# A fused LayerNorm, sliding-window attention and gated FFN kernel: 512-query chunks, a hand-set instruction order, resident weights, and the output projection summed in PSUM

## The chip, the cores and the metric

The kernel runs on one core of one Trainium2 chip. The metric is the device time of one execution in microseconds, and lower is better. A profile is of one execution, and the measured time lies about 2 us above its span (first to last instruction).

Engines are named as the profile names them: PE is TensorE, DVE VectorE, ACT ScalarE, POOL GpSimd and SP SyncE. PEclk is the clock that the throttle granted to PE, as a share of full speed.

## The reference, cut to what matters

One token sequence of 2048 x 512 is normalised. The result feeds windowed attention (32 heads of 16 columns, each query sees its own and the 255 preceding keys) and a gated FFN without a nonlinearity. Both halves and the input are summed. All tensors are bfloat16.

```python
def _layernorm(x, axis=-1, eps=1e-5):
    m = jnp.mean(x, axis=axis, keepdims=True)
    v = jnp.var(x, axis=axis, keepdims=True)
    return (x - m) / jnp.sqrt(v + eps)

def _A_ref(x, wqkv, wo):                      # wqkv (512, 1536), wo (512, 512)
    H = 32; Dh = D // H; W = 256
    ...
    mask = (idx[:, None] - idx[None, :] >= 0) & (idx[:, None] - idx[None, :] < W)
    scores = jnp.where(mask[None, None], scores * (Dh ** -0.5), -1e9)   # condensed
    p = _softmax(scores, axis=-1)
    ...                                        # p @ v, heads joined, @ wo

def _B_ref(x, w_gate, w_up, w_down):           # F = 1792
    return ((x @ w_gate) * (x @ w_up)) @ w_down          # condensed

xn = _layernorm(A_x)
return A_x + _A_ref(xn, A_wqkv, A_wo) + _B_ref(xn, B_w_gate, B_w_up, B_w_down)
```

## The kernel before

The attention walks over blocks of 128 keys. For each block, four heads at a time, it computes the scores of 128 keys against 384 queries, takes exp on ACT, and cuts the two triangular masks on POOL. The value matmuls follow one group later. LayerNorm, projection and FFN units are emitted between those steps. A scheduler of the framework decides the final order of each engine; attention has high priority. The code is condensed: cuts are marked by "...", and lines that only allocate tiles are left out.

```python
    def ln_stats_chunks(self, Tlist):           # four blocks of 128 rows at once
        ...
                nc.vector.bn_stats(out=st[:], in_=xc[:, b, :])
                nc.vector.bn_aggr(out=self.mv_all[:, tb, :], in_=st[:])
        nc.scalar.activation(out=std[:, tb0:tb1], in_=self.mv_all[:, tb0:tb1, 1], func=ACT.Sqrt, ...)
        nc.vector.reciprocal(out=self.rstd_all[:, tb0:tb1], in_=std[:, tb0:tb1])

    def lnproj_block(self, tb, xnT):            # Q and K: 128 matmul columns at a time
        ...
        for c in range(4):
            for k in range(4):
                nc.tensor.matmul(ps[:, c, :], lhsT=W[:, k, 128 * c:128 * c + 128],
                                 rhs=xnT[:, k, 128 * b:128 * b + 128], start=(k == 0), stop=(k == 3))
        nc.scalar.activation(out=self.Q[:, :, tok], in_=ps[:], func=ACT.Copy)
        ...

    def ffn_gu_group(self, T, xnT, hT, fg, gsize):   # weights loaded again for each chunk
        ...
        wg = self.wstream.tile([128, 4, 128 * gsize], BF16, tag="wg")
        nc.sync.dma_start(out=wg[:, :, 0:ncol], in_=self.B_wg[...])
        ...

    def ffn_down_block(self, T, hT, b):         # FFN half goes to DRAM
        ...
        nc.vector.tensor_tensor(out=y0[:], in0=psd[:], in1=xb[:], op=ALU.add)
        nc.sync.dma_start(out=self.y0_d[128 * tb:128 * tb + 128, :], in_=y0[:])

    def attn_scores_group(self, hp, t, c, par, km):
        Nq = min(384, self.S - 128 * t)
        S = self.psum.tile([128, 4, 512], F32, tag="S", name="S", bufs=1)
        for e in range(4):
            ...                                  # one matmul of Nq columns on 16 or 32 rows
            nc.tensor.matmul(S[:, e, 0:Nq], lhsT=lhsT, rhs=rhs, start=True, stop=True,
                             tile_position=(32 * e, 0))
        nc.scalar.activation(out=P[:, :, 0:Nq], in_=S[:, :, 0:Nq], func=ACT.Exp, scale=0.25)
        nc.gpsimd.affine_select(out=P[:, :, 0:128], ...)
        if Nq == 384:
            nc.gpsimd.affine_select(out=P[:, :, 256:384], ...)

    def final_block(self, tb):                  # attention half goes to DRAM
        ...
        nc.vector.tensor_copy(out=att[:], in_=outp[:])
        nc.sync.dma_start(out=self.attn_d[128 * tb:128 * tb + 128, :], in_=att[:])

    def combine_block(self, tb, e1=None, e2=None):   # both halves come back
        e1.dma_start(out=a[:], in_=self.attn_d[128 * tb:128 * tb + 128, :])
        e2.dma_start(out=y[:], in_=self.y0_d[128 * tb:128 * tb + 128, :])
        nc.vector.tensor_tensor(out=r[:], in0=a[:], in1=y[:], op=ALU.add)
        nc.sync.dma_start(out=self.out_flat[128 * tb:128 * tb + 128, :], in_=r[:])
    ...
                self.pending.append((hp, t, heads))
                if len(self.pending) > 1:        # values one group behind scores
                    self.attn_pv(*self.pending.pop(0))       # condensed
```

The softmax here doesn't subtract the row's maximum and nothing guards it: scores larger than these inputs give would overflow.

## Time and profile before

| | before |
|---|---|
| time, median of 3 runs | 375.51 us (374.96 to 377.72) |
| span of the profile | 372.9 us |
| PE busy | 309.6 us, 83% |
| first score matmul starts, last matmul ends | 29.05 us, 357.7 us |

The page gives the busy time of each engine, and then, for 40 slices of the span, the busy share in tenths (here the rows of PE and of its granted clock):

```profile
PE 309.6 (83%) x3340; PEld 161.4 (43%) x3392; DVE 186.6 (50%) x390; ACT 201.5 (54%) x170; POOL 154.9 (42%) x256
...
PE   0187888998998898889999999999999989999930
PEclk9999899999999999999999999999999999999985
```

PE is the busiest engine by far. It is not full in the first three slices and in the last two. In between the digits 8 are short waits. The clock is nearly full throughout.

A record's length overlaps its neighbours (a matmul of 512 columns is recorded with 378 ns, and the next one starts 215 ns after it), so PE's work is better read from start-to-start distances in the timeline: 215 ns for a matmul of 512 columns, 56 ns for 128 columns, 25 ns for a value matmul of 17 columns, and about 370 ns for a score group. Times the counts, that is about 291 us.

Among the groups of instructions (busy time, mean ns, then idle time before them and what ended it) two lines matter:

```profile
L209 ACT ACTIVATE P<-S 128x1536 bf16<-128x1536 f32 (+2 forms) x128 | 175.4, 1370 | 90.5 <-PE S L206 73.1
L236 PE MATMUL acc<-Vaug,P 128*128 128x17 bf16 x1440 | 60.8, 171 | 16.4 <-POOL P L210 12.8
```

ACT's exp waits for PE (73.1 of its 90.5 us of idle time), so ACT isn't the bound. The value matmuls make PE wait 16.4 us in all, mostly for POOL's mask.

The chain of waits shows the start and the end. Its columns are start, length and what the time was spent on:

```profile
1.84 14.99 DMA xc<-in_A_x_dram
...
353.74 2.05 DMA attn_d<-att
...
356.33 3.11 DMA a<-attn_d
...
366.39 3.35 DMA a<-attn_d
```

The load in the first line is that of the second input chunk, which lands at 16.8 us; the first chunk had landed by 4.2 us. DVE's timeline shows how PE comes to depend on it:

```profile
16.85 0.69 DVE L101 BATCH_NORM_STATS2 st<-xc 128x6 f32<-128x512 bf16 x1 [7.16 <-DMA xc<-in_A_x_dram]
```

The statistics of the second chunk stand in DVE's order ahead of the copy that PE's first projection needs, so DVE waits 7.16 us and PE 7.9 us. At the end the attention half of each block goes out to DRAM and comes back before the sum.

### The profile page before, as it was taken

What the parts mean: (1) busy time and instruction counts of PE and PEld (TensorE: products, weight loads), DVE (VectorE), ACT (ScalarE), POOL (GpSimd) and SP (SyncE); (2) the same over time, 40 slices, a digit from 0 to 9 for tenths busy, and PEclk for the clock granted to TensorE, in tenths of its full rate; (3) what the DMA queues carried; (4) which work ended last, traced back from release to release, by engine and by line L of the source; (5) the groups of instructions that cost most, each with busy time, mean ns of one, the idle gap of its engine ahead of it and who ended that gap; (6) DMA issues with size and microseconds to landing.
All of it is one profiled execution on the core that took longest, in us unless ns stands there. A gap on an engine that the chain in (4) does not pass through costs nothing.

```text
span 372.9 us, 8075 instructions
## 1 busy us (share of the span) xinstructions
PE 309.6 (83%) x3340; PEld 161.4 (43%) x3392; DVE 186.6 (50%) x390; ACT 201.5 (54%) x170; POOL 154.9 (42%) x256
## 2 busy tenths in 40 slices
PE   0187888998998898889999999999999989999930
PEld 0164654454554445554434444444434444454410
DVE  3265465454546323355556434665664466667421
ACT  1029788767772674657566666666675446520000
POOL 4002545555552442535445555455564445330011
PEclk9999899999999999999999999999999999999985
DMA  7930012122014001011243212422333364442254
GB/s 287 335 95 3 7 53 58 35 80 58 6 54 114 26 4 59 30 56 58 59 113 88 78 49 71 129 87 72 98 104 99 110 193 153 123 124 77 70 156 153
DMA packets 46196, 33.81 MB, mean 91 GB/s; under 512 B 2544, under 2 KB 44912, under 8 KB 46160
## 3 DMA queue, kind: packets, MB, share of 16 engines
q1 hardware_dynamic: 44592, 29.63, 26.6%
q0 software_dynamic: 848, 3.02, 2.5%
q10 hardware_dynamic: 720, 0.66, 0.6%
q8 instruction: 26, 0.43, 0.5%
q14 instruction: 10, 0.08, 0.1%
HBM read 27.00 MB, written 6.29 MB: 89 GB/s over the span
## 4 chain that ended last, share of the span: by engine, by line
PE 45%; ACT 23%; DMA 10%; POOL 9%; DVE 6%; issue 5%; SPq 1%; ACTq 0%; DVEq 0%; POOLq 0%
ACT P L209 20%; POOL P L210 8%; PE acc L236 8%; PE psu L171 8%; PE psg L165 7%; PE S L206 6%; PE psd L180 5%; DMA xc<-in_A_x_dram 5%; PE ps L126 3%; PE outp L265 3%; DMA attn_d<-att 2%; PE ps L132 2%; DMA a<-attn_d 2%; DVE att L268 2%; DMA xb<-in_A_x_dram 1%
## 5 line engine op out<-in xcount | busy, mean ns | idle before, releaser
L209 ACT ACTIVATE P<-S 128x1536 bf16<-128x1536 f32 (+2 forms) x128 | 175.4, 1370 | 90.5 <-PE S L206 73.1
L210 POOL TENSOR_SCALAR_AFFINE_SELECT P<-P 128x512 bf16<-128x512 bf16 x128 | 81.8, 639 | 180.3 <-ACT P L209 180.3
L236 PE MATMUL acc<-Vaug,P 128*128 128x17 bf16 x1440 | 60.8, 171 | 16.4 <-POOL P L210 12.8
L214 POOL TENSOR_SCALAR_AFFINE_SELECT P<-P 128x512 bf16<-128x512 bf16 x112 | 71.8, 641 | 0.0
L236 PEld LDWEIGHTS <-P 128*128 128x128 bf16 x1440 | 48.5, 96 | 47.7 <-POOL P L210 34.6
L168 DVE CAST gsb<-psg 128x512 bf16<-128x512 f32 x56 | 38.6, 690 | 27.1 <-PE psg L165 26.6
L301 DVE TENSOR_SCALAR km<-K,colO 128x128 bf16<-128x128 bf16 x64 | 22.7, 357 | 27.8 <-PE S L206 27.5
L165 PEld LDWEIGHTS <-wg 128*128 128x128 bf16 x224 | 19.7, 96 | 18.4 <-issue 1.6
L171 PEld LDWEIGHTS <-wu 128*128 128x128 bf16 x224 | 19.3, 96 | 17.8 <-issue 2.5
L128 ACT ACTIVATE Q<-ps 128x512 bf16<-128x512 f32 x16 | 9.5, 596 | 29.8 <-PE ps L126 29.6
L206 PE MATMUL S<-Q,K 16*128 16x384 bf16 (+2 forms) x256 | 22.7, 323 | 1.4 <-ACT P L209 0.9
L126 PEld LDWEIGHTS <-Wqkv 128*128 128x128 bf16 x256 | 16.0, 101 | 15.6 <-issue 12.4
L206 PE MATMUL S<-Q,km 32*128 32x384 bf16 (+2 forms) x256 | 21.9, 321 | 0.4 <-ACT P L209 0.3
L134 DVE CAST K<-ps 128x512 bf16<-128x512 f32 x16 | 11.0, 690 | 16.9 <-PE ps L132 16.9
L206 PEld LDWEIGHTS <-K 16*128 16x128 bf16 x256 | 7.8, 91 | 23.7 <-issue 21.9
L265 PE MATMUL outp<-Wo,oT 128*128 128x512 bf16 x61 | 17.0, 380 | 1.2 <-DVE oT L262 0.9
L247 DVE RECIPROCAL rz<-acc 128x16 f32<-128x16 f32 x32 | 8.2, 255 | 18.8 <-PE acc L236 18.7
L206 PEld LDWEIGHTS <-km 32*128 32x128 bf16 x256 | 7.3, 90 | 22.4 <-issue 20.9
L132 PEld LDWEIGHTS <-Wqkv 128*128 128x128 bf16 x256 | 16.6, 104 | 0.7 <-issue 0.7
L101 DVE BATCH_NORM_STATS2 st<-xc 128x6 f32<-128x512 bf16 x16 | 10.3, 673 | 11.5 <-DMA xc<-in_A_x_dram 11.4
L171 PE MATMUL psu<-xnT_359,wu 128*128 128x512 bf16 x52 | 15.6, 378 | 0.3
L171 PE MATMUL psu<-xnT_141,wu 128*128 128x512 bf16 x53 | 14.9, 377 | 1.0 <-DVE gsb L168 0.8
(84 smaller groups left out, 383.2 us busy)
## 6 DMA issues: line engine op xcount, KB each, us to landing
wg<-in_B_w_gate_dram SPq DMA_DIRECT2D x28, 256.0 KB, 2.9
wu<-in_B_w_up_dram SPq DMA_DIRECT2D x28, 256.0 KB, 3.0
xc<-in_A_x_dram SPq DMA_DIRECT2D x4, 512.0 KB, 3.5
xb<-in_A_x_dram SPq DMA_DIRECT2D x16, 128.0 KB, 2.2
attn_d<-att SPq DMA_DIRECT2D x16, 128.0 KB, 2.0
out_dram<-r SPq DMA_DIRECT2D x16, 128.0 KB, 2.2
Wd<-in_B_w_down_dram POOLq DMA_DIRECT2D x1, 1792.0 KB, 14.1
Wqkv<-in_A_wqkv_dram SPq DMA_DIRECT2D x1, 1536.0 KB, 9.5
```

The source lines that it names most:

```text
L126: nc.tensor.matmul(ps[:, c, :], lhsT=W[:, k, 128 * c:128 * c + 128], rhs=xnT[:, k, 128 * b:128 * b + 128], start=(k == 0), stop=(k == 3))
L132: nc.tensor.matmul(ps[:, c, :], lhsT=W[:, k, 512 + 128 * c:512 + 128 * c + 128], rhs=xnT[:, k, 128 * b:128 * b + 128], start=(k == 0), sto ...
L165: nc.tensor.matmul(psg[:], lhsT=wg[:, k, 128 * j:128 * j + 128], rhs=xnT[:, k, :], start=(k == 0), stop=(k == 3))
L168: nc.vector.tensor_copy(out=gsb[:], in_=psg[:])
L171: nc.tensor.matmul(psu[:], lhsT=wu[:, k, 128 * j:128 * j + 128], rhs=xnT[:, k, :], start=(k == 0), stop=(k == 3))
L206: nc.tensor.matmul(S[:, e, 0:Nq], lhsT=lhsT, rhs=rhs, start=True, stop=True, tile_position=(32 * e, 0))
L209: nc.scalar.activation(out=P[:, :, 0:Nq], in_=S[:, :, 0:Nq], func=ACT.Exp, scale=0.25)
L210: nc.gpsimd.affine_select(out=P[:, :, 0:128], in_=P[:, :, 0:128], pattern=[[0, 4], [1, 128]], compare_op=ALU.is_ge, fill=0.0, base=0, chan ...
L214: nc.gpsimd.affine_select(out=P[:, :, 256:384], in_=P[:, :, 256:384], pattern=[[0, 4], [-1, 128]], compare_op=ALU.is_gt, fill=0.0, base=0, ...
L236: nc.tensor.matmul(acc[:, s, 0:17], lhsT=Pk[:, ek, 128 * j:128 * j + 128], rhs=self.Vaug[:, kb, h, 0:17], start=(i == 0), stop=(i == len(k ...
L265: nc.tensor.matmul(outp[:], lhsT=oT[:, c, :], rhs=self.Wo[:, c, :], start=(c == 0), stop=(c == 3))
L301: nc.vector.tensor_scalar(out=km[:], in0=self.K[:, c, 128 * t:128 * t + 128], scalar1=self.colO[:, 0:1], scalar2=None, op0=ALU.mult)
```

## The change

The intent is a kernel that keeps everything on the chip and has its order set by hand:

- All weights and the input are loaded once (DMA reads fall from 27.0 to 9.7 MB).
- Queries go in chunks of 512. Q and K are projected 512 columns at a time, and Q's copy moves from ACT to DVE.
- A score group fills all 512 columns of the S tile with two parts of different key blocks, so there are 96 exp calls instead of 128.
- Values follow two groups behind scores.
- The output projection accumulates into the same PSUM bank as the down projection. One add and one store finish a block.
- LayerNorm's inverse root goes to POOL (a power of -0.5), so ACT loads its table once (1283 ns), where the kernel before loads one six times (7.7 us).
- The framework's scheduler is switched off. A list of filler work is dealt out between the attention steps.

The diff replaces nearly the whole file. This is its core, with cuts marked by "..."; lines that only allocate tiles are left out, and the comments are added here:

```diff
+GROUPS = (                       # (key block, first query block, last, column)
+    ((-2, 0, 0, 0), (0, 0, 2, 128)),
+    ((-1, 0, 1, 0), (2, 2, 3, 256)),
+    ((1, 1, 3, 0), (3, 3, 3, 384)),
+)
...
-        nc.scalar.activation(out=std[:, tb0:tb1], in_=self.mv_all[:, tb0:tb1, 1], func=ACT.Sqrt,
-                             bias=self.eps[:, 0:1], scale=1.0)
-        nc.vector.reciprocal(out=self.rstd_all[:, tb0:tb1], in_=std[:, tb0:tb1])
+    def norm(self, t):
+        nc.vector.bn_stats(out=st[:], in_=self.x[:, t, :])
+        nc.vector.bn_aggr(out=mv[:], in_=st[:])
+        nc.gpsimd.tensor_scalar(out=ve[:], in0=mv[:, 1:2], scalar1=1e-5, scalar2=None, op0=ALU.add)
+        nc.gpsimd.tensor_tensor(out=rs[:], in0=ve[:], in1=self.mhalf[:], op=ALU.pow)
+        nc.vector.tensor_scalar(out=xn[:], in0=self.x[:, t, :], scalar1=mv[:, 0:1], scalar2=rs[:, 0:1],
+                                op0=ALU.subtract, op1=ALU.mult)
+        return xn
...
+    def scores(self, T, c, par, i):
+        for kb, q0, q1, col in parts:
+            for e in range(4):
+                nc.tensor.matmul(S[:, e, col:col + n], ..., tile_position=(32 * e, 0), ...)
+        nc.scalar.activation(out=P[:, :, lo:hi], in_=S[:, :, lo:hi], func=ACT.Exp, scale=0.25)
...
-        nc.sync.dma_start(out=self.y0_d[128 * tb:128 * tb + 128, :], in_=y0[:])
...
-        e1.dma_start(out=a[:], in_=self.attn_d[128 * tb:128 * tb + 128, :])
+    def finish(self, T, b):
+        for c in range(4):
+            nc.tensor.matmul(self.psd[:], lhsT=self.OT[T][:, c, 128 * b:128 * b + 128],
+                             rhs=self.Wo[:, c, :], start=False, stop=(c == 3))
+        nc.vector.tensor_tensor(out=y[:], in0=self.psd[:], in1=self.x[:, t, :], op=ALU.add)
+        nc.sync.dma_start(out=self.out_d[128 * t:128 * t + 128, :], in_=y[:])
...
+        def norm(T):                       # a filler: all four norms, then all four transposes
+            for b in range(4):
+                t = 4 * T + b
+                def f(t=t):
+                    self.xns[t] = self.norm(t)
+                add(0, f, NG * T)
+            for b in range(4):
+                t = 4 * T + b
+                add(1, lambda t=t: self.norm_transpose(t, self.xns.pop(t)), NG * T)
...
+        for T in range(NCH):
+            if T:
+                dn(T - 1)
+            if T + 1 < NCH:
+                norm(T + 1)
+            gu(T)
+            if T + 1 < NCH:
+                project(T + 1)
+        dn(NCH - 1)
...
+        NCH, NG, LAG = self.NCH, 24, 2
+        for g, s in enumerate(steps):
+            self.scores(*s)
+            fill(half, g)                  # half: this step's share of the fillers
+            if g >= LAG:
+                self.values(*steps[g - LAG])
+            fill(total * done_w / sum(weight), g)
...
-    kb.run()
+    with tc.manual_schedule():
+        k.run()
```

## The prediction

> **What bounds the kernel now.** PE. The page gives PE 83% of a 372.9 us span, ACT 54%, DVE 50%, POOL 42%. From start-to-start spacings in the timeline: a 512-column matmul 215 ns, a 128-column one 56, a 17-column value matmul 25, and a score group of four 384-column matmuls about 370 (96 to enter, 12 to issue, 263 until the next matmul). Times the counts, PE needs about 290 us. The other 83: about 17 before 20 us (chain of waits: xc's landing), about 15 after the last matmul (round trips of attn_d and y_d through DRAM, one by one), about 50 in between, mostly score group to value matmul waiting for POOL and the LayerNorm/projection stretch from 20 to 80 us, where windows show PE 15 to 17 of 20 us busy.
>
> **What the change does to PE's work: almost nothing.** QK projection goes from 512 x 56 = 28.7 us to 128 x 215 = 27.5. Score groups go from 128 to 96 of two parts each: I estimate 0.5 us each, 45 us against 46. The rest stays. Sum about 289.
>
> **Other engines.** ACT: exp has as many elements; 1536 columns take 1.455 us, so 2048 should take about 1.88: 176 becomes about 171; six table loads (7.7, 1283 ns each[...]) become one; Q's 9.5 moves to DVE. DVE loses att (11), r (8) and km (23), gains Q (11) and Ko (about 7). None is the bound.
>
> **Where I expect gain.**
> - Start: first scores at about 18 us, not 29; PE has lost 12 there, not about 30.
> - Middle: value matmuls lag two groups, so their POOL waits go. A step has about 3.0 us of PE work, against a 2.6 us loop of scores and exp on one S buffer: PE-bound.
> - End: no DRAM trips; 3 to 4 us after the last matmul.
>
> **Where I expect it to give some back.**
> - The four norms of a chunk stand together in a hand-set order. Each is a DVE, POOL, DVE chain of about 2 us (0.67 statistics, 0.17, two small POOL ops, 0.44), and its POOL ops queue behind selects that wait for exp.[...] The transposes behind them then hold PE about 9 us, three times (after groups 3, 32 and 56), perhaps with a lower clock after: about 30 us.
> - Fillers run out at group 92, because a transpose of the last columns blocks the list: about 10 us of PE waiting, then 16 of down matmuls.
>
> Sum: 289 + 12 + 30 + 10 + 3.5 + small waits 0 to 8 = about 345 to 352 of span; the time is 2.6 above the span. I take **347 us, 326 to 366**. Faster by over 2%: 0.90; within 2%: 0.08; slower: 0.02.
>
> **What would show it.** PE work near 290; three PE holes of 8 to 10 us ending in a wait on DVE xn; first scores near 18 us; one table load; PE nearly solid in the last 20 us.
>
> **What would make it wrong.** Norm bursts cheaper (small POOL ops overlapping, DVE running ahead) would give 320 to 330. Two-part score groups much dearer[...], or a slow pow on POOL, 360 and more.

What it says of the holes was in part an estimate. Of the 2 us for one norm, the trace of the kernel before shows 1.28 (0.67 + 0.17 + 0.44); the rest, for POOL's two operations and the hand-overs, was the author's guess (a whole cycle measured 2.23). That the engines keep the set order was an assumption; the profile after shows it for DVE. The lower clock after a hole, a "perhaps" in it, is measured below: 0.50 right after the first two.

## More of the kernel before

I cut the span at the first score matmul and at the last matmul. The columns of this view are: stretch, its length, busy time (and instructions) of PE, PEld, DVE, ACT and POOL, PEclk, DMA share and GB/s.

```profile
0.00:29.05 29.05, 10.57 (x110) 8.56 (x112) 12.78 (x38) 4.84 (x9) 3.83 (x11) 1.00 0.71 231
29.05:357.70 328.65, 299.04 (x3230) 152.85 (x3280) 170.97 (x347) 196.61 (x162) 149.10 (x242) 0.99 0.26 75
357.70:372.90 15.20, 0.00 (x0) 0.00 (x0) 2.82 (x6) 0.00 (x0) 1.95 (x4) 0.59 0.52 155
```

PE idles 29.05 - 10.57 = 18.5 us at the start, 29.6 us in the middle and 15.2 us at the end.

## The result, and the profile after

| | before | after |
|---|---|---|
| time, median of 4 fast runs of the same round | 376.32 us (374.96 to 377.72) | 352.36 us (352.09 to 353.01) |
| ratio (95% interval) | | 0.937 (0.934 to 0.940) |
| span of the profile | 372.9 us | 351.3 us |
| first score matmul, last matmul | 29.05, 357.7 us | 22.26, 348.0 us |

A ratio here is the mean time of one kernel's fast runs over that of the other's in the same rounds, so it isn't quite the ratio of the medians that I quote. The outputs were correct. The prediction was 347 us (326 to 366).

The same rows of the page, and the same three stretches:

```profile
PE 303.1 (86%) x3200; PEld 143.2 (41%) x3200; DVE 167.2 (48%) x323; ACT 179.6 (51%) x114; POOL 160.3 (46%) x281
...
PE   2783599999899379999989729999999999996696
PEclk9999599999999769999999967999999999999599
```

```profile
0.00:22.26 22.26, 12.52 (x41) 4.26 (x41) 8.58 (x22) 3.88 (x6) 4.95 (x17) 1.00 0.96 324
22.26:348.00 325.74, 290.55 (x3160) 138.99 (x3159) 157.99 (x301) 175.73 (x108) 155.35 (x264) 0.94 0.05 15
348.00:351.30 3.30, 0.00 (x0) 0.00 (x0) 0.68 (x1) 0.00 (x0) 0.00 (x0) 1.00 0.11 40
```

The span is 21.6 us shorter. The start gives 29.05 - 22.26 = 6.8 us of it and the end 15.2 - 3.3 = 11.9 us. The middle, which most of the change is about, gives only 2.9 us. PE's idle time in it even grew, from 29.6 to 35.2 us, and its clock fell from 0.99 to 0.94.

The row of PE shows why. It is no longer evenly filled. There are three dents (digits 3 and 5, 3, 7 and 2), each with a dent in PEclk. Here are the two groups of PE's instructions that had the waits:

```profile
L196 PE MATMUL acc<-V,P 128*128 128x17 bf16 x1440 | 51.0, 171 | 2.4 <-POOL P L176 2.0
L120 PE MATMUL xTp<-ident,xn 128*128 128x128 bf16 x64 | 9.2, 292 | 32.9 <-DVE xn L109 26.7
```

The wait of the value matmuls went from 16.4 to 2.4 us, as the longer lag intended (a_lag1 below asks how much of this is the lag's). A new wait stands in its place: the transposes of the normalised rows wait 32.9 us. This is PE's timeline at the second dent (start, length, instruction, and in brackets the idle time before it and what ended it):

```profile
115.54 0.55 PE L196 MATMUL acc<-V,P 128*128 128x17 bf16 x16
119.11 0.46 PE L120 MATMUL xTp<-ident,xn 128*128 128x128 bf16 x4 [3.02 <-DVE xn L109]
121.34 0.61 PE L120 MATMUL xTp<-ident,xn 128*128 128x128 bf16 x4 [1.77 <-DVE xn L109]
123.57 0.61 PE L120 MATMUL xTp<-ident,xn 128*128 128x128 bf16 x4 [1.62 <-DVE xn L109]
126.13 0.61 PE L120 MATMUL xTp<-ident,xn 128*128 128x128 bf16 x4 [1.96 <-DVE xnT_1557 L121]
...
127.22 1.89 PE L225 MATMUL gp<-xnT_357,Wg 128*128 128x512 bf16 x4
128.90 0.62 PE L196 MATMUL acc<-V,P 128*128 128x17 bf16 x16
```

PE does nothing but sixteen short transposes from 116 to 126.7 us; it idles 8.4 us of that. The other two holes are alike: 9.4 us from 29.5 and 8.4 us from 200. Together that is 26.1 us. After the hole the four gate matmuls start 0.42 us apart, (128.90 - 127.22) / 4, where full speed is 0.215; the granted clock from 127.2 to 129.0 us is 0.50. So the clock is halved for a while.

DVE's timeline shows what PE waits for (the POOL operations fall in the gaps of 1.0 us):

```profile
118.64 0.41 DVE L109 TENSOR_SCALAR xn<-x,mv,rs 128x512 bf16<-128x512 bf16 x1 [1.40 <-POOL rs L107]
118.97 0.69 DVE L101 BATCH_NORM_STATS2 st<-x 128x6 f32<-128x512 bf16 x1
119.69 0.18 DVE L103 BATCH_NORM_AGGREGATE mv<-st 128x2 f32<-128x6 f32 x1
120.87 0.41 DVE L109 TENSOR_SCALAR xn<-x,mv,rs 128x512 bf16<-128x512 bf16 x1 [1.00 <-POOL rs L107]
...
125.33 0.41 DVE L109 TENSOR_SCALAR xn<-x,mv,rs 128x512 bf16<-128x512 bf16 x1 [1.00 <-POOL rs L107]
125.66 1.54 DVE L121 COPY xnT_1557<-xTp 128x512 bf16<-128x512 bf16 x4
```

One row block takes 2.23 us (118.64 to 120.87): statistics, aggregate, a trip to POOL for an add of 0.22 us and a power of 0.57 us, and the scaling. DVE doesn't begin the next block's statistics while it waits: it idles 1.40 us before the first scaling, and the statistics that stand behind this scaling in the program start 0.33 us after it (118.97), though the rows they read were loaded long before (the last load of x was issued at 8.64 us, and none of its loads took over 14.8 us to land). In all four row blocks DVE keeps the order of the program.

The last bracket in PE's timeline is of a second kind. The transposes have three PSUM buffers. The fourth needs the first one back, and its copy stands behind the fourth scaling in DVE's order, so all four copies run together at 125.66. Most of these 1.96 us would have been waited for the fourth scaling anyway: it starts at 125.33, and the other transposes start 0.47 us after their scaling starts, which would be 125.80 here. They start at 126.13, so the buffer costs about 0.3 us per hole. I hadn't foreseen it.

The clock falls with the holes. In the first hole the longest single wait is 4.14 us, in this one 3.02 us, with only transposes between the waits; right after both, the matmuls of 512 columns start 0.42 us apart at a granted clock of 0.50. At the end of the list it falls too: it is 0.50 from 325 to 330 us, after two waits of 1.57 us with score and value matmuls between them. How long a wait it takes isn't shown, since no run here tests it. The table of stretches shows the granted clock:

```profile
60.00:115.00 55.00, 53.82 (x594) 25.49 (x591) 25.52 (x48) 36.12 (x26) 29.21 (x48) 1.00 0.03 9
115.00:127.00 12.00, 3.63 (x44) 2.04 (x41) 6.69 (x17) 0.88 (x1) 4.95 (x11) 0.68 0.03 11
127.00:140.00 13.00, 13.00 (x140) 5.91 (x136) 7.04 (x13) 7.51 (x4) 5.99 (x10) 0.90 0.01 1
```

From 60 to 115 us, between the first two holes, PE is busy 53.8 of 55 us, at full clock. So the new design reached its aim in the steady state, and lost the gain in three places.

### The profile page after: what moved, and what is told of

The parts are those of the page before. It is cut to its first block, busy times and chain, and to the rows that moved or that the text cites. A ratio compares the mean times of both kernels' runs of the same rounds, so it can differ in the third digit from the quotient of the medians.

```text
span 351.3 us, 7407 instructions
## 1 busy us (share of the span) xinstructions
PE 303.1 (86%) x3200; PEld 143.2 (41%) x3200; DVE 167.2 (48%) x323; ACT 179.6 (51%) x114; POOL 160.3 (46%) x281
## 3 DMA queue, kind: packets, MB, share of 16 engines
q10 hardware_dynamic: 1584, 1.57, 1.4%
## 4 chain that ended last, share of the span: by engine, by line
PE 79%; DVE 9%; POOL 6%; ACT 3%; issue 2%; DMA 1%; POOLq 0%; ACTq 0%
PE gp L225 15%; PE up L234 15%; PE psd L243 14%; PE acc L196 9%; PE S L163 8%; PE qkp L138 8%; PE vp L128 4%; PE psd L250 4%; ACT P L171 3%; POOL rs L107 3%; DVE st L101 2%; DVE xn L109 2%; PE xTp L120 1%; POOL P L176 1%; POOL ve L105 1%
## 5 line engine op out<-in xcount | busy, mean ns | idle before, releaser
L171 ACT ACTIVATE P<-S 128x2048 bf16<-128x2048 f32 (+2 forms) x96 | 170.0, 1771 | 130.1 <-PE S L163 122.3
L196 PE MATMUL acc<-V,P 128*128 128x17 bf16 x1440 | 51.0, 171 | 2.4 <-POOL P L176 2.0
L228 DVE CAST gsb<-gp 128x512 bf16<-128x512 f32 x56 | 38.7, 691 | 27.0 <-PE gp L225 27.0
L120 PE MATMUL xTp<-ident,xn 128*128 128x128 bf16 x64 | 9.2, 292 | 32.9 <-DVE xn L109 26.7
L253 DVE TENSOR_TENSOR y<-psd,x 128x512 bf16<-128x512 f32 x16 | 11.1, 692 | 55.3 <-PE psd L250 55.3
L225 PEld LDWEIGHTS <-Wg 128*128 128x128 bf16 x224 | 18.6, 99 | 21.6 <-issue 7.0
L234 PEld LDWEIGHTS <-Wu 128*128 128x128 bf16 x224 | 18.4, 98 | 20.5 <-issue 5.5
L138 PEld LDWEIGHTS <-Wqkv 128*128 128x128 bf16 x128 | 10.9, 99 | 13.1 <-issue 4.1
L225 PE MATMUL gp<-xnT_1557,Wg 128*128 128x512 bf16 x56 | 15.3, 398 | 0.0
L225 PE MATMUL gp<-xnT_132,Wg 128*128 128x512 bf16 x56 | 15.3, 397 | 0.0
L225 PE MATMUL gp<-xnT_357,Wg 128*128 128x512 bf16 x56 | 15.3, 397 | 0.0
L234 PE MATMUL up<-xnT_1557,Wu 128*128 128x512 bf16 x56 | 15.3, 397 | 0.0
L243 PE MATMUL psd<-Wd,hT_3897 128*128 128x512 bf16 x56 | 14.8, 423 | 0.0
L234 PE MATMUL up<-xnT_132,Wu 128*128 128x512 bf16 x56 | 14.7, 385 | 0.0
## 6 DMA issues: line engine op xcount, KB each, us to landing
x<-in_A_x_dram SPq DMA_DIRECT2D x1, 1024.0 KB, 14.8
```

The lines of the kernel that those rows point to most:

```text
L120: nc.tensor.transpose(ps[:, k, :], xn[:, 128 * k:128 * k + 128], self.ident[:])
L138: nc.tensor.matmul(ps[:], lhsT=self.Wqkv[:, k, lo:lo + 128], rhs=self.xnT[T][:, k, :], start=(k == 0), stop=(k == 3))
L171: nc.scalar.activation(out=P[:, :, lo:hi], in_=S[:, :, lo:hi], func=ACT.Exp, scale=0.25)
L196: nc.tensor.matmul(acc[:, q, e, 0:17], lhsT=P[:, e, j:j + 128], rhs=self.V[:, 4 * T + kb, 8 * c + 2 * e + par, 0:17], start=(first and n = ...
L225: nc.tensor.matmul(ps[:], lhsT=self.Wg[:, k, 128 * f:128 * f + 128], rhs=self.xnT[T][:, k, :], start=(k == 0), stop=(k == 3))
L228: nc.vector.tensor_copy(out=self.gsb[:], in_=ps[:])
```

## The experiments

My theory after this reading was: the order of the four norms in one burst costs the new kernel about 30 us, part as idle time and part as clock. The rivals were that the rest of the loss lies in the attention steps themselves (score groups in two parts, the lag), or that a hand-set order is worse than the scheduler's in general. The other runs price single parts of the change. Each run was compared with the kernel before on the same chip in the same rounds; to compare two versions across rounds I use their ratios to it. The prices are those in a kernel that still has its three holes, so they needn't add up. Runs of three rounds are meant if nothing else is said.

### a_spread: the norms moved between the gate and up matmuls

The arithmetic stays the same. The norm is cut into statistics, scaling and transposes, which are emitted between the fillers of the current chunk, so that neither DVE nor PE waits for POOL's trip.

```diff
-            if T + 1 < NCH:
-                norm(T + 1)
             gu(T)
...
             for f in range(NF):
                 add(4, lambda f=f: self.gate(T, f))
                 add(4, lambda f=f: self.up(T, f))
+                if T + 1 < NCH:
+                    for b in range(4):
+                        t = 4 * T + 4 + b
+                        if f == 2 * b:        # bn_stats, bn_aggr, both POOL operations
+                            add(0, lambda t=t: stats(t), NG * (T + 1))
+                        if f == 2 * b + 3:    # the scaling
+                            add(0, lambda t=t: apply(t), NG * (T + 1))
+                        if f == 2 * b + 5:    # the four transposes and the copy
+                            add(1, lambda t=t: self.norm_transpose(t, self.xns.pop(t)), NG * (T + 1))
```

> The kernel after, with the LayerNorm of the next chunk cut into three pieces (statistics and the two POOL ops; the scaling; the transposes) and spread through the gate/up fillers instead of standing in one burst; the prologue is untouched. Theory (PE held by the serial DVE, POOL, DVE chain in strict program order): the three PE holes at 29 to 41, 116 to 126 and 200 to 211 us vanish, PE's idle time before the transposes falls from 32.9 us to under 5, the clock's dips there go too, and the time falls by 25 to 32 us, to 320 to 328. Rival (the holes are only moved: DVE or the three PSUM banks are the true limit, and PE waits elsewhere instead): the time stays above 343.

Measured: 318.52 us (318.26 to 319.24), ratio 0.849 (0.845 to 0.853). That is 0.906 of the changed kernel's ratio, 33 to 34 us less, slightly more than the 25 to 32 us I expected. The page's rows and the middle stretch:

```profile
PE   2789999999899999999899999999999999994795
PEclk9999999999999999999999999999999999997699
```

```profile
21.48:313.20 291.72, 278.43 (x3104) 136.77 (x3159) 154.96 (x300) 175.74 (x108) 155.63 (x264) 0.98 0.06 18
```

The three dents are gone. The middle shrank from 325.7 to 291.7 us, which is 34.0. PE's busy time in it fell by 12.1 us for the same matmuls, and its idle time by 21.9 us. The first number is what the low clock had cost; the clock rose from 0.94 to 0.98. The split is rough, since 56 matmul records of this trace are missing, but the sum is not. The burst was the cause.

### a_onetrip: the burst kept, but one trip to POOL for four row blocks

If the trips were the cost of a burst, one trip instead of four should give back part of it.

```diff
+        for b in range(4):
+            nc.vector.bn_stats(out=st[:], in_=self.x[:, 4 * T + b, :])
+            nc.vector.bn_aggr(out=mv4[:, b, :], in_=st[:])
+        nc.gpsimd.tensor_scalar(out=ve4[:], in0=mv4[:, :, 1], scalar1=1e-5, scalar2=None, op0=ALU.add)
+        nc.gpsimd.tensor_tensor(out=rs4[:], in0=ve4[:], in1=self.mhalf[:, 0:1].to_broadcast([128, 4]), op=ALU.pow)
+        for b in range(4):
+            ...                                # the four scalings
```

> The kernel after, burst kept in its place, but the four tiles of a chunk make one round trip to POOL (two ops of 128x4) instead of four (eight ops of 128x1). Theory of the serial chain: of each hole the first wait (3 to 4 us, POOL's queue of selects) stays, the three further waits of 1.4 to 1.8 us go, so each hole of about 8 to 9.5 us of idle falls to about 4.5 to 6, and the time falls by 9 to 15 us, to 337 to 343. Rival (POOL's queue of selects alone makes the hole): under 4 us of gain.

Measured: 343.59 us (342.85 to 344.31), ratio 0.915 (0.911 to 0.919), some 8 us less than the changed kernel. PE's timeline at the second hole has one wait in place of four:

```profile
118.41 2.06 PE L138 MATMUL xTp<-ident,xn 128*128 128x128 bf16 x16 [5.51 <-DVE xn L127]
```

The three holes now wait 5.85, 5.51 and 5.88 us, 17.2 in all instead of 26.1. The gain is about the 9 us of waiting, and falls just short of the 9 to 15 us I expected. The holes lie at the upper end of the 4.5 to 6 us that I gave them; one reason may be that POOL's power of 128x4 takes 1.05 us where a single one takes 0.57. So a shorter chain in one piece still leaves a hole here. Work between its links closes it: in a_spread the transposes wait 6.5 us for scalings, in four places, as many as the prologue of the changed kernel has by itself.

### a_auto: the changed kernel with the framework's scheduler

```diff
-    with tc.manual_schedule():
-        k.run()
+    k.run()
```

> The kernel after without its hand-set order: the framework's own scheduler orders the instructions of each engine, as it did in the kernel before; everything else is the same. If the hand-set order is what made the kernel faster, it loses most of the gain: 362 or more. If the order costs more (three holes) than it gives, because the scheduler can put other work into the holes: 330 to 348, and PE's idle before the transposes falls below 15 us. I lean to the second, without much confidence.

Measured: 324.64 us (324.02 to 324.87), ratio 0.866 (0.863 to 0.869). With the same instructions the scheduler's order is about 27 us faster than the order by hand, and faster than either range I had written. It does by itself what a_spread does. DVE's timeline at the first chunk border:

```profile
26.20 0.67 DVE L142 CAST K<-qkp 128x512 bf16<-128x512 f32 x1
26.79 0.17 DVE L103 BATCH_NORM_AGGREGATE mv<-st 128x2 f32<-128x6 f32 x1
26.88 0.66 DVE L101 BATCH_NORM_STATS2 st<-x 128x6 f32<-128x512 bf16 x1
...
36.45 0.69 DVE L228 CAST gsb<-gp 128x512 bf16<-128x512 f32 x1
37.06 0.40 DVE L109 TENSOR_SCALAR xn<-x,mv,rs 128x512 bf16<-128x512 bf16 x1
```

The statistics run early, between K's copies, and the scalings stand between the FFN's copies. So the hand-set order as such was a loss in this kernel, for this one place. The scheduler's start is worse, though: its first score matmul comes at 25.8 us, not at 22.3.

### a_spread_auto: a_spread with the scheduler

This asks whether the hand order is worth anything once the burst is gone. The edit is the one of a_auto, made to a_spread.

> The spread kernel under the framework's own scheduler instead of the hand-set order. With the burst, the scheduler's order was 28 us faster than the hand-set one (324.6 against 352.4). If the burst was the only thing wrong with the hand-set order, then without it the hand-set order is as good or better: this kernel takes 317 to 326, and not less than the hand-ordered 318.5. If the scheduler is better in other ways too, it comes under 312.

Measured: 323.24 us (320.77 to 325.45), ratio 0.858 (0.852 to 0.865). Against a_spread's ratio of 0.849 the hand order is about 1% better here, with intervals that just touch. So in this kernel the hand-set order isn't worse once the burst is gone, and the rival falls.

### a_lag1: values one group behind scores, as before

```diff
-        NCH, NG, LAG = self.NCH, 24, 2
+        NCH, NG, LAG = self.NCH, 24, 1
```

> The kernel after with value matmuls one group behind the scores instead of two. My prediction said that the lag of two takes away the waits of the value matmuls on POOL (16.4 us of idle before). If the lag is what did it, PE idle before the value matmuls rises from 2.4 us to 10 or more and the time by 5 to 15 us. Rival (the waits are gone because every step has enough filler work between scores and values, whatever the lag): idle stays under 6 us and the time within 2% of the kernel after (348 to 358).

Measured: 357.96 us (356.1 to 358.95), ratio 0.952 (0.947 to 0.957), 5.6 us slower than the changed kernel. The group of value matmuls:

```profile
L196 PE MATMUL acc<-V,P 128*128 128x17 bf16 x1440 | 54.8, 171 | 8.1 <-POOL P L176 4.8 <-POOL P L180 1.4
```

Its wait goes from 2.4 back to 8.1 us, which is as much as the time that was lost. It doesn't reach the 16.4 us of before, and lies between the 10 us or more of the theory and the under 6 us of the rival. So the lag accounts for about 6 of the 14 us by which this wait fell; the rest belongs to other parts of the new order, which I didn't separate.

### a_g384: score groups of 384 columns, as before

The new groups, but in four pieces of 384 columns (120 groups in place of 96). The rest of the edit, not shown, fits the fillers' step numbers to the larger count.

```diff
-    ((-2, 0, 0, 0), (0, 0, 2, 128)),
-    ((-1, 0, 1, 0), (2, 2, 3, 256)),
-    ((1, 1, 3, 0), (3, 3, 3, 384)),
+    ((0, 0, 2, 0),),
+    ((-2, 0, 0, 0), (-1, 0, 1, 128)),
+    ((1, 1, 3, 0),),
+    ((2, 2, 3, 0), (3, 3, 3, 256)),
```

> The kernel after with score groups of 384 columns as before, four to a chunk, head set and parity (120 groups) instead of full banks of 512 (96 groups). Theory: a group costs PE about 200 ns to enter and leave whatever its size, and ACT about 175 ns; 24 more groups cost 4 to 6 us of PE: 356 to 359. Rival (group size is immaterial since PE is hidden by other work or the holes take it up): within 1.5 us of the kernel after.

Measured: 366.70 us (365.57 to 367.77), ratio 0.977 (0.972 to 0.982), 14 us slower than the changed kernel where I expected 4 to 6. One part shows in the list of PE's waits (total, times, longest):

```profile
PE S L164 <- ACT P L172: 9.6, 20, 1.2
```

In the changed kernel this wait was 3.3 us in 3 places. With more and smaller groups, the loop of score, exp, score on the single S buffer binds in 20 places. I estimate the entries into score groups at 24 x 0.2 us, from the 0.2 us that a group costs beyond its columns (in the changed kernel 0.1 us to enter, then 0.22, 0.27 and 0.33 us until the next matmul for 256, 384 and 512 columns, which leaves 0.1 without columns): 5 us. The sum is 11 us, and the clock is lower, 0.930 against 0.942. I underestimated full groups: I had counted entries and not the buffer loop. How much is clock stays open.

### a_wo_apart: the output projection in its own PSUM bank

```diff
-            nc.tensor.matmul(self.psd[:], lhsT=self.OT[T][:, c, ...], rhs=self.Wo[:, c, :], start=False, stop=(c == 3))
+            nc.tensor.matmul(wop[:], lhsT=self.OT[T][:, c, ...], rhs=self.Wo[:, c, :], start=(c == 0), stop=(c == 3))
+        nc.vector.tensor_copy(out=att[:], in_=wop[:])
+        nc.vector.tensor_tensor(out=y[:], in0=att[:], in1=y0[:], op=ALU.add)
```

> The kernel after with the output projection in its own PSUM bank, copied out and added by DVE (two more DVE ops for each 128 rows, 16 x (0.69 + 0.48) = 18.7 us of DVE) instead of summed onto the down projection. Theory: DVE has slack and PE's matmuls are the same, so only the end grows: 0 to 4 us, 352 to 357. Rival (the sum in PSUM is a main source of the gain): 360 or more.

Measured: 353.31 us (352.72 to 355.57), ratio 0.944 (0.940 to 0.948). Against the changed kernel's 0.937 (0.934 to 0.940), the sum in PSUM is worth a few microseconds at most, as expected. It takes work from DVE, which isn't the bound (48% busy in the changed kernel).

### a_stream: gate and up weights loaded again for each chunk, as before

```diff
+        if f % 2 == 0:
+            self.wgt = self.wstream.tile([128, 4, 256], BF16, tag="wg", name="wg")
+            nc.sync.dma_start(out=self.wgt[:], in_=self.wg_v[:, :, 128 * f:128 * f + 256])
+            ...                                # the same for the up weights
```

> The kernel after with gate and up weights loaded again for each chunk, 256 columns at a time into two buffers, as before, instead of resident. Theory: PE waits for no DMA in either kernel apart from the start, so the time stays within 3 us of the kernel after. Rival (less DMA traffic is what made it faster): 360 or more.

Measured: 361.06 us (359.83 to 361.5), ratio 0.963 (0.960 to 0.966), 9 us slower. I had held that PE waits for no weights, since DMA moves little. In one place it does. SP's timeline around 270 us, and PE's wait:

```profile
269.97 16.57 SPq L256 DMA_DIRECT2D out_dram<-y  x4
286.64 0.39 SPq L221 DMA_DIRECT2D wg<-in_B_w_gate_dram  x1
```

```profile
PE gp L227 <- DMA wg<-in_B_w_gate_dram: 4.0, 1, 4.0
```

In the order of SP the loads for the next chunk come after four stores of results. Each store waits for its result; the four are spread over 16.6 us, and the load is issued only after the fourth. PE waits 4.0 us and then runs at a clock of 0.53 from 290 to 295 us, which I estimate at another 2.3 us (0.47 of 5). The rest of the 9 us I didn't trace. Bandwidth isn't scarce there: the DMA share is 0.48 and then 0.37. So the larger part of what resident weights save in this kernel is a late load and the low clock after it, not bytes.

### b_sbuf: the kernel before, with the attention half kept on the chip

The copy of the attention half goes into a slot of SBUF that is dead by then, and the last chunk's FFN half stays in SBUF too.

```diff
-        nc.vector.tensor_copy(out=att[:], in_=outp[:])
-        nc.sync.dma_start(out=self.attn_d[128 * tb:128 * tb + 128, :], in_=att[:])
+        nc.vector.tensor_copy(out=self.o_all[:, tb, :], in_=outp[:])
...
-        nc.vector.tensor_tensor(out=r[:], in0=a[:], in1=y[:], op=ALU.add)
+        nc.vector.tensor_tensor(out=r[:], in0=self.o_all[:, tb, :], in1=yy, op=ALU.add)
```

> The kernel before with one part of the change alone: the attention half of the output stays in SBUF (in a dead slot of o_all), and the FFN half of the last chunk too, so nothing at the end goes through DRAM and back. Theory: the stretch after the last matmul, 15 us, falls to about 5, and the time by 8 to 11 us, to 364 to 368. Rival (the end would be as long for other reasons, such as the last loads of x): under 4 us.

Measured: 367.37 us (366.23 to 370.03), ratio 0.981 (0.976 to 0.986). The stretch after the last matmul:

```profile
364.20:368.30 4.10, 0.05 (x1) 0.00 (x0) 1.12 (x2) 0.00 (x0) 0.00 (x0) 0.92 0.09 32
```

It is 4.1 us instead of 15.2. In this profile the last matmul came later (364.2 against 357.7); that profiled run was also the slowest of the four. The end of the change can be had alone, for about 2% of the time (7 to 8 us, just under the 8 to 11 expected).

### b_xc1: the kernel before, with the second input chunk loaded ahead of the QKV weights

```diff
         self.get_xc(0)
+        self.get_xc(1)
         Wqkv = big.tile([128, 4, 3 * 512], BF16, name="Wqkv")
```

> The kernel before with one line moved: the load of the second chunk of x is issued right after the first, ahead of Wqkv. In the trace of before, DVE's statistics of chunk 1 stand ahead of the copy that PE waits for, and wait for that load until 16.85 us; PE is idle 7.9 us. Theory: the load lands near 7 us, PE's first projection starts at about 12 to 13 instead of 17.9 (Wqkv then lands somewhat later, near 12), and the time falls by 4 to 6 us, to 369 to 371. Rival (the start is bound by Wqkv or by DMA bandwidth in all): within 2 us of before.

I expected 4 to 6 us from it. Measured: 374.97 us as the median of all four runs (373.24 to 375.42 for the three fast ones), ratio of fast runs 0.996 (0.992 to 1.001): the same. One of the four runs, the one with the profile, was slow: 572.31 us. From that profile I read only the order of the waits. The chain of waits at the start goes over the weights now, not over the input:

```profile
1.83 14.20 DMA Wqkv<-in_A_wqkv_dram
...
16.08 2.43 PE ps L127 x16
```

It suggests that the start waits for all that was loaded first, whichever comes last. Since it is a slow run, this stays an argument and isn't shown. What made the run slow isn't shown either: around 300 us three matmuls of 512 columns start 443 ns apart (299.69 to 301.02 us), about twice the usual 215, while the granted clock was recorded as 1.0.

### a_best: a_spread with three more edits

These were a new start (one POOL trip for the first four row blocks, K and Q ahead of V), a new end (the last chunk's first down block ahead of the transpose that holds up the list) and a slower pace of fillers, to keep some for the end.

```diff
+        self.norm_first()                      # one trip for four row blocks
-        for lo in (1024, 512, 0):              # order of the QKV weights: V, K, Q
+        for lo in (512, 0, 1024):              # K, Q, V
+                if last and c == 3:
+                    block(0)
-        total = sum(w[0] for w in work) - 40
+        total = sum(w[0] for w in work) - 73
```

> The spread kernel (318.5 us) with two more changes: the prologue makes one trip to POOL for the first four tiles and computes K and Q before V (V becomes filler work, the weights' pieces are loaded in that order); and at the end the fillers are paced to last until the last group, with the first down block of the last chunk put ahead of the transpose that waits for the last values. Theory: first scores at about 14 us instead of 22 with V's 3.4 us still to do, so 4 to 6 us gained at the start; PE's waits after group 92 (about 8 us of idle and a dip of the clock) nearly vanish, 5 to 9 us gained: 304 to 310. Rival (start and end are bound by the loads and by the exp chain, not by the order): above 314.

Measured: 324.04 us (323.5 to 325.86), ratio 0.863 (0.860 to 0.867). I expected 304 to 310, and it is slower than a_spread. PE's list of waits shows two of the reasons:

```profile
PE xTp L138 <- DVE xn L127: 14.7, 4, 12.2
...
PE S L181 <- DVE Q L166: 3.5, 4, 0.9
```

The one trip waits for all four row blocks to land, so the first transposes wait 12.2 us. The first score matmul comes at 21.45 us, as early as in a_spread (21.48), but V's projection is still to be done. With the slower pace the K and Q projections are only made when the chunk border forces them, and the scores wait for Q there. The end itself came as meant: after 280 us PE waits once, for 0.8 us. But scores wait for exp earlier instead, 6.6 us in six places.

### a_end: a_spread with the new end alone (five rounds)

```diff
             for c in range(4):
+                if last and c == 3:
+                    block(0)
                 add(1, lambda c=c: self.o_transpose(T, c), None, NG * T + 6 * c + 5)
```

> The spread kernel (318.5 us, ratio 0.849) with one further edit: in the last chunk the first down block (14 matmuls, 3 us) stands ahead of the transpose that waits for the last values, so that it is there to fill the end; prologue and pacing are those of the spread kernel. In the spread kernel PE idles there 1.57, 1.56 and 1.70 us, then 0.8, and the clock is low for a while after. Theory: 3 of those 5.6 us of idle go, and the dip of the clock with them: 312 to 316, ratio 0.832 to 0.843. Rival (the end is bound by exp and the selects, or the clock dips anyway): ratio within 0.006 of 0.849.

Measured: 317.91 us (317.33 to 318.5, six runs), ratio 0.846 (0.843 to 0.849). That misses the main expectation, 0.832 to 0.843, and fits the rival (within 0.006 of 0.849). One of the two waits of the last scores for exp is gone (1.6 us), the others stay, and the dent of the clock moves rather than vanishes. The gain over a_spread is about 1 us, and the intervals overlap.

The fastest kernels are a_end and a_spread, at 318 us: 15% below the kernel before and 10% below the changed one.

## Why the prediction was right or wrong, point by point

The prediction was right: 352.4 us lies in its range, 1.5% above its centre, and the change was faster. (Its sum, with the 2.6 us above the span, gives 348 to 355 us; the stated centre lies just under that.) This is its sum, beside what the profile shows. PE's work is an estimate from start-to-start distances times counts; what the middle has beyond it is PE's idle time, and the rest, 13.6 us, I put down to the lower clock. That is a remainder and not measured by itself; a_spread's drop of 12.1 us in busy time is of the same size.

| term | predicted | measured |
|---|---|---|
| PE's work | 289 | about 283 |
| start, beyond PE's work | 12 | 16 (22.3 less 6.0 of work) |
| three holes, with the clock after them | 30 | 26.1 idle, and most of 13.6 of lower clock |
| end of the list | 10 | 5.7 idle, and some of that clock |
| small waits | 0 to 8 | about 3 |
| after the last matmul | 3.5 | 3.3 |
| sum | 345 to 352 | 351.3 |

- **The burst of norms** was the main mechanism, and right. The holes were foreseen as three of about 9 us, and they measured 9.4, 8.4 and 8.4. a_spread took them away and gained 34 us: with the clock the burst cost slightly more than the 30 us predicted. Two things in it were not foreseen. The fourth transpose waits some 0.3 us more for a PSUM buffer, as worked out above. And POOL's operations queue behind the masks less than I had said: DVE waits 2.17, 1.40 and 1.00 us for the first power of the three holes, and 1.00 us for each later one. So the queue cost about 1.2 us in the first hole, where the masks wait for an exp, 0.4 in the second and nothing in the third.
- **PE's work** was overestimated because of the score groups. I took 0.5 us for a group in two parts. This timeline of the changed kernel shows one, between two FFN pieces:

```profile
144.85 1.02 PE L225 MATMUL gp<-xnT_357,Wg 128*128 128x512 bf16 x4
145.81 0.40 PE L163 MATMUL S<-Q_1037,Ko 32*128 32x128 bf16 x8
146.13 1.04 PE L234 MATMUL up<-xnT_357,Wu 128*128 128x512 bf16 x4
```

  The four gate matmuls need 0.86 us at 0.215 each, and the group starts after 0.96: 0.1 us to enter. From its start to the next matmul it is 0.32 us, so 0.42 in all. The second part adds its columns and no wait that shows: in the same trace the next matmul starts 0.22 us after a group of 256 columns in one part (63.21 us), 0.27 after one of 384 in one part (60.90) and 0.33 after one of 512 in two (64.78), about 0.055 us for each 128 columns.
- **The start** was mis-sized. I said 18 us for the first scores; it was 22.3. A row block of the prologue takes 3.35 us, in one chain over DVE, POOL and PE, and the projections after it ran at half speed: 512 columns took 0.42 us from start to start (16.93 to 18.61 us for four), though the profile's PEclk reads 1.00 there. It cost 4 us more than the term said. The two errors, 6 us of PE's work too much and 4 us of start too little, nearly cancel, and that is luck.
- **The middle** was PE-bound outside the holes, as predicted (53.8 of 55 us before the second hole), and the wait of the value matmuls fell from 16.4 to 2.4 us. I gave the lag as the reason; a_lag1 shows it for about 6 of these 14 us.
- **The end** came as said: 3.3 us after the last matmul. The list of fillers runs out, PE waits between 320 and 330 us (1.57 and 1.57 for exp, 1.70 for POOL, 0.81 for DVE, 5.7 in all and not 10), and then the down matmuls follow without a gap. The first 14 of them take 5.1 us, the next 14 take 3.0, so the low clock adds about 2 us.
- **ACT** was right: exp took 170.0 us in all (171 predicted), and its table load comes once, at 1283 ns.

What stays open: how the cost of 384-column groups splits between buffer loop and clock; what beside the lag cut the wait of the value matmuls; and what binds the start of the kernel before.

## What to carry to other kernels

When an order is set by hand and the engines keep to it, as DVE did here while it waited 1.40 us for POOL, a chain over several engines must not stand as one block in front of work that is ready: cut it at each hand-over and put independent work between the pieces (33 to 34 us in this kernel). A busy share averaged over the span hides such holes, so cut the profile at its events (first score, last matmul, dents in the row of PE) and ask of each stretch what it gained. Where a scheduler is at hand, one run with it tells in minutes whether an order by hand has a hole.
